# Linear attention and dense layers on one core: the query phase by token halves

## The chip, the cores and the metric

The kernel runs on one core of one Trainium2 chip. The core has a matrix engine (TensorE, PE in the profile, with its weight loads as PEld), a vector engine (VectorE, DVE), an engine for functions of one operand (ScalarE, ACT), a general engine (GpSimd, POOL) and an engine that issues transfers (SyncE, SP). Matrix products land in PSUM, which the kernel divides into eight tiles of 128 x 512; everything else is in SBUF, 128 partitions wide. The metric is the device time of one execution in microseconds (us), given as the median of the runs.

## What is computed

The reference is a linear attention followed by two dense layers, all in float32.

```python
def phi(x):                                   # per head; 128 features from 64 values
    proj = x @ w_phi
    proj = proj - max(abs(proj), axis=-1)     # one maximum per token
    return concat(exp(proj), exp(-proj))      # 256 features

kv  = phi(k).T @ v                            # per head 256 x 64
z   = sum(phi(k), axis=tokens)                # per head 256
num = phi(q) @ kv
den = phi(q) @ z + 1e-6
x   = num / den                               # 8 batches x 576 tokens, 8 heads x 64 = 512 values
out = leaky_relu(x @ w_in, 0.01) @ w_out      # 4608 tokens, 512 -> 2048 -> 512
```

Note that the subtraction uses the largest absolute value of a token's 128 projections, and that it is the same number for both signs of the exponent.

## The kernel before

**Pairs.** Attention goes by pairs of heads. A batch has 8 heads, so 4 pairs, and there are 32 pairs; pair i belongs to batch i // 4. Pairs 0 to 3 (batch 0) go through code of their own at the start (`first_k_phase`, `first_q_phase`); the others through `k_phase(i)` and `q_phase(i)`. The key phase builds the pair's key-value matrix in five chunks of tokens (tiles kvh and, from pair 8 on, kvl, each with one buffer). The query phase projects the queries, subtracts the maxima, takes the exponentials, multiplies by the key-value matrix and divides by the denominators. Its result goes into `ring`, a tile with two batch slots.

**High and low parts.** From pair 8 on, and in the dense layers throughout, a float32 operand is split into a rounded part and the rest (names ending in h and l), and a product is the sum of three matmuls in a faster format. The query phase rounds its exponentials with a reduction over one element (L378, tile qh) and takes the rest on POOL (line 72, tile ql).

**The dense layers.** They go by 18 blocks of 256 tokens. `split` reads a block's input out of `ring` with casts on ScalarE (tile xh, line 67) and subtractions on POOL (tile xl, line 72); the casts are cut where a batch ends, so a block's pieces have 64, 128, 192 or 256 columns. `layer1` is 12 matmuls for each of 16 slices of the hidden layer (L572, L573, L575), `layer2` is 6 (L592 to L594). Blocks 0 and 1 run interleaved while the weights still arrive. Block 1 keeps its low part in a buffer that the key phase's value tile vhl takes over from pair 8 on.

**The query phase in detail (L321 to L402).** A pair has two heads j and 576 tokens, in two halves u of U = 288.

1. Four projections, each 288 tokens of a head, land in PSUM (tag a, three buffers, which key phase and query phase share). VectorE transposes each into the tile tq (L346). This transpose works in blocks of 32 by 32, so that a token's 128 features lie in four groups of 32 partitions.
2. For each head a reduction (L348) takes the maxima over the 32 features that a partition sees: tile m, 18 blocks of tokens.
3. The four groups must be combined. Four transfers from SP bring the four groups side by side into a tile ms of 32 partitions (L351), VectorE reduces them to mm (L354), and four transfers bring the result to all four groups as mx (L357).
4. For each head: subtract (L364), transpose back into mb (L366), then for each half both exponentials (L371, L372), the rounding, the matmuls with the key-value matrix (L386, L388, L391) into a PSUM tile, and two copies on ScalarE: the numerator into `ring` (L393), the denominator into a part of tq that is no longer needed (L394, `dn = tq[:, 0]`).
5. When both heads and both halves are through: transpose the denominators (L397), reciprocal (L399), transpose back (L400), and one multiply on POOL over 576 columns of `ring` (line 72, ring from ring and mb).

The denominator comes in 64 equal rows per head, which is why one column per block of 32 serves for the reciprocal.

**What sets the order.** `attention()` runs `k_phase(i)` and `q_phase(i - 1)` as two generators that take turns; each `yield` ends a turn. `advance` draws on that stream between the slices of the dense layers. This writes the program's order and gives each instruction a priority: attention's stands ahead of the dense layers', weights' preparation in between. The tile framework then makes, when the kernel is built, one fixed order for each engine from priorities, dependences, free buffers and a model of durations. On the chip each engine works its list in that order and waits where an operand is late. A tile with one buffer can only be taken again when everything that reads it is over. `BUFS` holds the buffer counts of SBUF tags; tags not named there have one.

```python
BUFS = {"kph": 2, "eq": 2, "m4": 2, "g": 2, "gh": 2, "gl": 2, "qh": 2, "ql": 2}
PBUFS = {"a": 3, "c": 1, "h": 2, "acc": 2}
```

Of the kernel before, what the change touches and what calls it, by code (L numbers as in the profile page):

```python
# [17 lines left out]
P = 128  # L18
# [13 lines left out]
NK = 8  # L32
BUFS = {"kph": 2, "eq": 2, "m4": 2, "g": 2, "gh": 2, "gl": 2, "qh": 2, "ql": 2}
PBUFS = {"a": 3, "c": 1, "h": 2, "acc": 2}
# [10 lines left out]
def attention_moe_kernel(ctx: ExitStack, tc: tile.TileContext, q, k, v, vt, w_phi, w_in, w_out, out):  # L45
# [275 lines left out]
    def q_phase(i):  # L321
# [12 lines left out]
        tq = st([P, 2, 2, U], F32, "tq")  # L334
        m = st([P, 2, 18], F32, "m")
        for j in range(2):
            for u in range(2):
                pq = pt("a")[:, 0:U]
                us = slice(U * u, U * u + U)
                if nat:  # L340
                    r = slice(64 * j, 64 * j + 64)
                    nc.tensor.matmul(pq, lhsT=bd[r, F * j : F * j + F], rhs=rq[r, us], start=True, stop=True)
                else:
                    nc.tensor.matmul(pq, lhsT=wq_h, rhs=qs[:, j, us], start=True, stop=False)  # L344
                    nc.tensor.matmul(pq, lhsT=wq_l, rhs=qs[:, j, us], start=False, stop=True)  # L345
                nc.vector.transpose(tq[:, j, u], pq)  # L346
                yield
            nc.vector.tensor_reduce(m[:, j], blocks(tq[:, j]), axis=AX.X, op=ALU.max, apply_absolute_value=True)  # L348
        ms = st([32, 4, 2, 18], F32, "ms")
        for a in range(4):  # L350
            nc.sync.dma_start(ms[:, a], m[32 * a : 32 * a + 32])  # L351
        yield
        mm = st([32, 2, 18], F32, "mm")
        nc.vector.tensor_reduce(mm, ms.rearrange("p a j c -> p j c a"), axis=AX.X, op=ALU.max)  # L354
        mx = st([P, 2, 18], F32, "mx")
        for a in range(4):
            nc.sync.dma_start(mx[32 * a : 32 * a + 32], mm)  # L357
        m = mx
        yield
        kvh, kvl = kvs_of[i]  # L360
        dn = tq[:, 0]
        for j in range(2):
            tj = blocks(tq[:, j])
            nc.vector.tensor_tensor(tj, tj, m[:, j].unsqueeze(2).broadcast_to([P, 18, 32]), op=ALU.subtract)  # L364
            mb = st([P, 2, U], F32, "mb")
            nc.vector.transpose(mb.rearrange("p a b -> p (a b)"), tq[:, j].rearrange("p a b -> p (a b)"))  # L366
            yield
            es = []
            for u in range(2):
                eq = st([P, 2, U], F32, "eq")  # L370
                nc.scalar.activation(eq[:, 0], mb[:, u], AF.Exp)  # L371
                nc.scalar.activation(eq[:, 1], mb[:, u], AF.Exp, scale=-1.0)  # L372
                if nat:
# [7 lines left out]
                yield  # L381
            for u in range(2):
                qh, ql = es[u]
                nm = pt("a")[:, 0:U]
# [7 lines left out]
                rr = slice(64 * j, 64 * j + 64)  # L392
                nc.scalar.copy(ring[rr, b % 2, hp, U * u : U * u + U], nm[0:64])  # L393
                nc.scalar.activation(dn[rr, u], nm[64:128], AF.Copy, bias=1e-6)  # L394
                yield
        dt = st([P, 2, U], F32, "mb")
        nc.vector.transpose(dt.rearrange("p a b -> p (a b)"), dn.rearrange("p a b -> p (a b)"))  # L397
        rc = st([P, 18], F32, "rc")
        nc.vector.reciprocal(rc, blocks(dt)[:, :, 0])  # L399
        nc.vector.transpose(blocks(dt), rc.unsqueeze(2).broadcast_to([P, 18, 32]))  # L400
        x = ring[:, b % 2, hp]
        tt_("x", x, x, dt.rearrange("p a b -> p (a b)"), ALU.mult)  # L402
        yield

# [284 lines left out]
```

## Time and profile before

| What | Value |
| --- | --- |
| Median of 3 runs | 1220.52 us (1220.07 to 1224.94) |
| Profiled execution, first to last instruction (span) | 1217.5 us; the page gives no other time for it |
| Mean granted TensorE clock | 0.989 |
| TensorE matmuls | busy 1171.4 us, 96%, 7496 matmuls |
| TensorE weight loads | busy 1038.5 us, 85% |
| ScalarE | busy 865.7 us, 71% |
| VectorE | busy 741.7 us, 61% |
| GpSimd | busy 625.2 us, 51% |

How to read it. The first number of a timeline row is the start in us from the first instruction, the second the duration in us, then engine, source line, operation, the tile written and the tiles read, sizes and count; in brackets stand the idle time before it and what ended that. Matmuls are pipelined: the durations of neighbours overlap, so the number of matmuls in a stretch says more than their busy time. PEclk is the clock that TensorE was granted, as a share of full speed. Line 67 and line 72 are helpers that serve many tiles: there one goes by the tile names. In a row of waits the numbers are the total in us, how many times, and the longest.

### The profile page before, as it was taken

To read this page: it belongs to the slowest core of one execution; us is meant where nothing else is said; L and a number is where in the kernel's file an instruction comes from. 1 tells how busy PE (TensorE), PEld (TensorE's weight loads), DVE (VectorE), ACT (ScalarE), POOL (GpSimd) and SP (SyncE) were. 2 spreads that over 40 slices of the span, in tenths; PEclk is the share of its full clock that TensorE was granted. 3 is DMA by queue.
4 is the path that set the end of the run, shared out by engine and by line. 5 is a ranking of instruction groups with operands and counts; after the bars stand their busy time and mean duration, and the time that the engine had idled before them with its cause. 6 is when DMAs were issued, how large, how long until landed. Compare 5 with 4: busy or idle time off the path is not lost.

```text
span 1217.5 us, 21546 instructions
## 1 busy us (share of the span) xinstructions
PE 1171.4 (96%) x7496; PEld 1038.5 (85%) x7496; DVE 741.7 (61%) x1243; ACT 865.7 (71%) x2267; POOL 625.2 (51%) x681
## 2 busy tenths in 40 slices
PE   8889999789998999989999999999999999999998
PEld 5577778579996999879999999899999999989997
DVE  6969893556677666667667766776776766400000
ACT  5977785677877777877878887887887877533232
POOL 0132222355766566655757666766676757433232
PEclk9999999899999999989999999999999999999999
DMA  7526241201111011111101010111111110000000
GB/s 213 149 73 167 86 116 32 75 24 33 50 25 56 13 32 40 42 41 33 49 23 49 22 50 22 50 33 49 33 39 29 43 23 19 3 18 1 18 18 18
DMA packets 73532, 58.07 MB, mean 48 GB/s; under 512 B 55888, under 2 KB 57040, under 8 KB 73424
## 3 DMA queue, kind: packets, MB, share of 16 engines
q1 hardware_dynamic: 73424, 56.70, 16.7%
q8 instruction: 59, 0.97, 0.3%
q14 instruction: 49, 0.40, 0.1%
HBM read 46.20 MB, written 9.44 MB: 46 GB/s over the span
## 4 chain that ended last, share of the span: by engine, by line
PE 72%; ACT 8%; DVE 6%; issue 4%; DMA 3%; POOL 3%; SPq 2%; DVEq 0%; POOLq 0%; ACTq 0%
PE h L572 9%; PE h L575 9%; PE h L573 9%; PE acc L592 8%; PE acc L593 8%; PE acc L594 8%; PE c L224 6%; PE a L386 2%; PE a L244 2%; PE a L391 2%; PE a L388 2%; DMA ring<-in_w_in_dram 1%; DMA ms<-m 1%; PE a L344 1%; PE a L345 1%
## 5 line engine op out<-in xcount | busy, mean ns | idle before, releaser
L72 POOL TENSOR_TENSOR gl<-g,gh 128x256 fp32r<-128x256 f32 x288 | 233.7, 816 | 314.7 <-ACT gh L67 251.9
L572 PE MATMUL h<-xh,w0h 128*128 128x256 f32 x1088 | 281.3, 286 | 7.4 <-ACT xh L67 4.1
L573 PE MATMUL h<-xh,w0l 128*128 128x256 f32 x1088 | 278.2, 283 | 0.0
L572 PEld LDWEIGHTS h<-xh,w0h 128*128 128x128 f32 x1088 | 206.9, 190 | 20.4 <-ACT xh L67 5.1
L592 PE MATMUL acc<-w1h,gh 128*128 128x512 f32 x544 | 215.7, 396 | 0.0
L573 PEld LDWEIGHTS h<-xh,w0l 128*128 128x128 f32 x1088 | 207.1, 190 | 9.1
L593 PE MATMUL acc<-w1l,gh 128*128 128x512 f32 x544 | 214.8, 395 | 0.0
L594 PE MATMUL acc<-w1h,gl 128*128 128x512 f32 x544 | 204.2, 397 | 0.1
L575 PE MATMUL h<-xl,w0h 128*128 128x256 f32 x1088 | 192.2, 283 | 0.0
L579 ACT ACTIVATE g<-h 128x256 f32<-128x256 f32 x288 | 108.1, 380 | 97.3 <-PE h L575 84.2
L72 POOL TENSOR_TENSOR ql<-eq,qh 128x576 fp32r<-128x576 f32 x96 | 146.7, 1537 | 51.6 <-DVE qh L378 39.3
L67 ACT CAST gh<-g 128x256 fp32r<-128x256 f32 x288 | 114.5, 403 | 65.0 <-PE acc L593 62.8
L575 PEld LDWEIGHTS h<-xl,w0h 128*128 128x128 f32 x1088 | 157.4, 190 | 0.9 <-issue 0.4
L72 POOL TENSOR_TENSOR kpl<-ek,kph 128x512 fp32r<-128x512 f32 x72 | 97.2, 1350 | 80.2 <-ACT kph L67 46.5
L269 ACT ACTIVATE ek<-pmk,m4n 128x128 f32<-128x128 f32 (+1 forms) x240 | 88.4, 393 | 44.4 <-POOL kpl L72 23.1
L594 PEld LDWEIGHTS acc<-w1h,gl 128*128 128x128 f32 x544 | 99.9, 188 | 18.7 <-POOL gl L72 0.9
L592 PEld LDWEIGHTS acc<-w1h,gh 128*128 128x128 f32 x544 | 102.5, 188 | 13.7 <-issue 0.8
L593 PEld LDWEIGHTS acc<-w1l,gh 128*128 128x128 f32 x544 | 102.5, 189 | 12.6
L270 ACT ACTIVATE ek<-pmk,m 128x128 f32<-128x128 f32 (+1 forms) x240 | 88.0, 391 | 25.3 <-DVE m L252 20.8
L378 DVE TENSOR_REDUCE qh<-eq 128x576 fp32r<-128x576 f32 x96 | 70.0, 750 | 42.6 <-ACT eq L372 23.3
L224 PE MATMUL c<-kph,vhl 128*66 128x256 f32 (+1 forms) x480 | 78.0, 285 | 5.3 <-ACT kph L67 5.1
L249 DVE TENSOR_TENSOR pmk<-a,pmk 128x256 f32<-128x256 f32 (+1 forms) x120 | 48.3, 417 | 50.5 <-ACT pmk L67 47.9
(201 smaller groups left out, 2324.8 us busy)
## 6 DMA issues: line engine op xcount, KB each, us to landing
out_dram<-o SPq DMA_DIRECT2D x35, 256.0 KB, 2.0
rq<-in_q_dram SPq DMA_DIRECT2D x28, 288.0 KB, 2.9
rk<-in_k_dram SPq DMA_DIRECT2D x27, 288.0 KB, 2.8
rv<-in_v_dram SPq DMA_DIRECT2D x29, 256.0 KB, 3.5
ring<-in_w_in_dram SPq DMA_DIRECT2D x9, 512.0 KB, 3.8
f<-in_w_out_dram SPq DMA_DIRECT2D x7, 512.0 KB, 3.6
f<-in_w_in_dram SPq DMA_DIRECT2D x7, 512.0 KB, 3.7
ring<-in_w_out_dram SPq DMA_DIRECT2D x5, 512.0 KB, 3.7
```

What stands on the lines that cost most here:

```text
L67: nc.scalar.copy(o, i)
L72: (nc.vector if pick(key) == "v" else nc.gpsimd).tensor_tensor(o, a, b, op=op)
L224: nc.tensor.matmul(kvp[0 : lt.shape[1], 256 * j : 256 * j + 256], lhsT=lt, rhs=rt, start=first and j == 0, stop=last, skip_group_check=True)
L269: nc.scalar.activation(ek[r, j, 0:F], pmk[r, h], AF.Exp, bias=m4n[r, h : h + 1])
L270: nc.scalar.activation(ek[r, j, F:256], pmk[r, h], AF.Exp, scale=-1.0, bias=m4[r, h : h + 1])
L572: nc.tensor.matmul(ph, lhsT=weight(0, "h", ft)[:, d * P : d * P + P], rhs=xh[d], start=d == 0, stop=False)
L573: nc.tensor.matmul(ph, lhsT=weight(0, "l", ft)[:, d * P : d * P + P], rhs=xh[d], start=False, stop=False)
L575: nc.tensor.matmul(ph, lhsT=weight(0, "h", ft)[:, d * P : d * P + P], rhs=xl[d], start=False, stop=d == NP - 1)
L579: nc.scalar.activation(g, ph, AF.Prelu, alpha=0.01)
L592: nc.tensor.matmul(a, lhsT=gh[:, ts], rhs=weight(1, "h", ft), start=ft == 0, stop=False)
L593: nc.tensor.matmul(a, lhsT=gh[:, ts], rhs=weight(1, "l", ft), start=False, stop=False)
L594: nc.tensor.matmul(a, lhsT=gl[:, ts], rhs=weight(1, "h", ft), start=False, stop=ft == NFT - 1)
```

## The change

The query phase changes in four places.

- **Order.** Where it went head by head and, within a head, half by half, it now goes half by half and, within a half, both heads. tq is laid out with the half outermost, and the reductions, subtractions and transposes take a half of both heads (2 x 288 columns, the same size as before).
- **Denominators.** They get a tile of their own (dn, 288 columns, now two buffers) and are no longer written into tq. The tail (transpose, reciprocal, transpose, multiply on POOL) runs once for each half over 288 columns and not once for the pair over 576; the transposed denominators take the other buffer of dn and not mb.
- **Crossing of the maxima.** m has room for four groups. The group that already lies in partitions 0 to 31 stays where it is; three transfers bring the others beside it, the reduction writes straight into partitions 0 to 31 of mx, and three transfers bring it to the other groups. The tiles ms and mm are gone.
- **Scratch.** The argument `dynamic_dma_scratch_size` goes from 1024 to 256.

```diff
-BUFS = {"kph": 2, "eq": 2, "m4": 2, "g": 2, "gh": 2, "gl": 2, "qh": 2, "ql": 2}
+BUFS = {"kph": 2, "eq": 2, "m4": 2, "g": 2, "gh": 2, "gl": 2, "qh": 2, "ql": 2, "dn": 2}
...
-        m = st([P, 2, 18], F32, "m")
-        for j in range(2):
-            for u in range(2):
+        m = st([P, 4, 2, 18], F32, "m")
+        for u in range(2):
+            us = slice(U * u, U * u + U)
+            for j in range(2):
...
-                nc.vector.transpose(tq[:, j, u], pq)
+                nc.vector.transpose(tq[:, u, j], pq)
                 yield
-            nc.vector.tensor_reduce(m[:, j], blocks(tq[:, j]), axis=AX.X, op=ALU.max, apply_absolute_value=True)
-        ms = st([32, 4, 2, 18], F32, "ms")
-        for a in range(4):
-            nc.sync.dma_start(ms[:, a], m[32 * a : 32 * a + 32])
-        yield
-        mm = st([32, 2, 18], F32, "mm")
-        nc.vector.tensor_reduce(mm, ms.rearrange("p a j c -> p j c a"), axis=AX.X, op=ALU.max)
+            nc.vector.tensor_reduce(m[:, 0, u], blocks(tq[:, u]), axis=AX.X, op=ALU.max, apply_absolute_value=True)
+        for a in range(1, 4):
+            nc.sync.dma_start(m[0:32, a], m[32 * a : 32 * a + 32, 0])
+        yield
         mx = st([P, 2, 18], F32, "mx")
-        for a in range(4):
-            nc.sync.dma_start(mx[32 * a : 32 * a + 32], mm)
-        m = mx
+        nc.vector.tensor_reduce(mx[0:32], m[0:32].rearrange("p a u c -> p u c a"), axis=AX.X, op=ALU.max)
+        for a in range(1, 4):
+            nc.sync.dma_start(mx[32 * a : 32 * a + 32], mx[0:32])
         yield
         kvh, kvl = kvs_of[i]
-        dn = tq[:, 0]
-        for j in range(2):
-            tj = blocks(tq[:, j])
-            nc.vector.tensor_tensor(tj, tj, m[:, j].unsqueeze(2).broadcast_to([P, 18, 32]), op=ALU.subtract)
+        for u in range(2):
+            us = slice(U * u, U * u + U)
+            tu = blocks(tq[:, u])
+            nc.vector.tensor_tensor(tu, tu, mx[:, u].unsqueeze(2).broadcast_to([P, 18, 32]), op=ALU.subtract)
             mb = st([P, 2, U], F32, "mb")
-            nc.vector.transpose(mb.rearrange("p a b -> p (a b)"), tq[:, j].rearrange("p a b -> p (a b)"))
+            nc.vector.transpose(mb.rearrange("p a b -> p (a b)"), tq[:, u].rearrange("p a b -> p (a b)"))
             yield
             es = []
-            for u in range(2):
+            for j in range(2):
                 eq = st([P, 2, U], F32, "eq")
-                nc.scalar.activation(eq[:, 0], mb[:, u], AF.Exp)
+                nc.scalar.activation(eq[:, 0], mb[:, j], AF.Exp)
...
-            for u in range(2):
-                qh, ql = es[u]
+            dn = st([P, U], F32, "dn")
+            for j in range(2):
+                qh, ql = es[j]
...
-                nc.scalar.copy(ring[rr, b % 2, hp, U * u : U * u + U], nm[0:64])
-                nc.scalar.activation(dn[rr, u], nm[64:128], AF.Copy, bias=1e-6)
+                nc.scalar.copy(ring[rr, b % 2, hp, us], nm[0:64])
+                nc.scalar.activation(dn[rr], nm[64:128], AF.Copy, bias=1e-6)
                 yield
-        dt = st([P, 2, U], F32, "mb")
-        nc.vector.transpose(dt.rearrange("p a b -> p (a b)"), dn.rearrange("p a b -> p (a b)"))
-        rc = st([P, 18], F32, "rc")
-        nc.vector.reciprocal(rc, blocks(dt)[:, :, 0])
-        nc.vector.transpose(blocks(dt), rc.unsqueeze(2).broadcast_to([P, 18, 32]))
-        x = ring[:, b % 2, hp]
-        tt_("x", x, x, dt.rearrange("p a b -> p (a b)"), ALU.mult)
-        yield
+            dt = st([P, U], F32, "dn")
+            nc.vector.transpose(dt, dn)
+            dt = dt.rearrange("p (c d) -> p c d", d=32)
+            rc = st([P, 9], F32, "rc")
+            nc.vector.reciprocal(rc, dt[:, :, 0])
+            nc.vector.transpose(dt, rc.unsqueeze(2).broadcast_to([P, 9, 32]))
+            x = ring[:, b % 2, hp, us]
+            tt_("x", x, x, dt.rearrange("p c d -> p (c d)"), ALU.mult)
+            yield
...
-    nc = _bacc.Bacc("TRN2", target_bir_lowering=False, num_devices=1, dynamic_dma_scratch_size=1024)
+    nc = _bacc.Bacc("TRN2", target_bir_lowering=False, num_devices=1, dynamic_dma_scratch_size=256)
```

More of the change, by code (lines that the diff above doesn't have):

```diff
@@ L334, in q_phase @@
         tq = st([P, 2, 2, U], F32, "tq")
-        m = st([P, 2, 18], F32, "m")
-        for j in range(2):
-            for u in range(2):
+        m = st([P, 4, 2, 18], F32, "m")
+        for u in range(2):
+            us = slice(U * u, U * u + U)
+            for j in range(2):
                 pq = pt("a")[:, 0:U]
-                us = slice(U * u, U * u + U)
                 if nat:
@@ L345, in q_phase @@
                     nc.tensor.matmul(pq, lhsT=wq_l, rhs=qs[:, j, us], start=False, stop=True)
-                nc.vector.transpose(tq[:, j, u], pq)
+                nc.vector.transpose(tq[:, u, j], pq)
                 yield
-            nc.vector.tensor_reduce(m[:, j], blocks(tq[:, j]), axis=AX.X, op=ALU.max, apply_absolute_value=True)
-        ms = st([32, 4, 2, 18], F32, "ms")
-        for a in range(4):
-            nc.sync.dma_start(ms[:, a], m[32 * a : 32 * a + 32])
+            nc.vector.tensor_reduce(m[:, 0, u], blocks(tq[:, u]), axis=AX.X, op=ALU.max, apply_absolute_value=True)
+        for a in range(1, 4):
+            nc.sync.dma_start(m[0:32, a], m[32 * a : 32 * a + 32, 0])
         yield
-        mm = st([32, 2, 18], F32, "mm")
-        nc.vector.tensor_reduce(mm, ms.rearrange("p a j c -> p j c a"), axis=AX.X, op=ALU.max)
         mx = st([P, 2, 18], F32, "mx")
-        for a in range(4):
-            nc.sync.dma_start(mx[32 * a : 32 * a + 32], mm)
-        m = mx
+        nc.vector.tensor_reduce(mx[0:32], m[0:32].rearrange("p a u c -> p u c a"), axis=AX.X, op=ALU.max)
+        for a in range(1, 4):
+            nc.sync.dma_start(mx[32 * a : 32 * a + 32], mx[0:32])
         yield
         kvh, kvl = kvs_of[i]
-        dn = tq[:, 0]
-        for j in range(2):
-            tj = blocks(tq[:, j])
-            nc.vector.tensor_tensor(tj, tj, m[:, j].unsqueeze(2).broadcast_to([P, 18, 32]), op=ALU.subtract)
+        for u in range(2):
+            us = slice(U * u, U * u + U)
+            tu = blocks(tq[:, u])
+            nc.vector.tensor_tensor(tu, tu, mx[:, u].unsqueeze(2).broadcast_to([P, 18, 32]), op=ALU.subtract)
             mb = st([P, 2, U], F32, "mb")
-            nc.vector.transpose(mb.rearrange("p a b -> p (a b)"), tq[:, j].rearrange("p a b -> p (a b)"))
+            nc.vector.transpose(mb.rearrange("p a b -> p (a b)"), tq[:, u].rearrange("p a b -> p (a b)"))
             yield
             es = []
-            for u in range(2):
+            for j in range(2):
                 eq = st([P, 2, U], F32, "eq")
-                nc.scalar.activation(eq[:, 0], mb[:, u], AF.Exp)
-                nc.scalar.activation(eq[:, 1], mb[:, u], AF.Exp, scale=-1.0)
+                nc.scalar.activation(eq[:, 0], mb[:, j], AF.Exp)
+                nc.scalar.activation(eq[:, 1], mb[:, j], AF.Exp, scale=-1.0)
                 if nat:
```

## The prediction

> **What bounds the kernel now.** I read the page's busy shares first, then a table of stretches, then the order of work in the stretches that fall short.
>
> ```profile
> PE 1171.4 (96%) x7496; PEld 1038.5 (85%) x7496; DVE 741.7 (61%) x1243; ACT 865.7 (71%) x2267; POOL 625.2 (51%) x681
> ```
> ```profile
> core 0: us, PE busy (x) PEld busy (x) DVE busy (x) ACT busy (x) POOL busy (x), PEclk, DMA share, GB/s
> 220.00:260.00 40.00, 28.39 (x138) 21.88 (x138) 22.26 (x42) 28.87 (x75) 13.16 (x15) 0.83 0.27 74
> 370.00:400.00 30.00, 23.94 (x141) 20.04 (x141) 19.17 (x35) 22.60 (x60) 16.82 (x19) 0.94 0.17 50
> 510.00:540.00 30.00, 22.92 (x124) 19.54 (x125) 20.72 (x36) 23.81 (x63) 16.41 (x16) 0.83 0.18 51
> 600.00:1000.00 400.00, 399.65 (x2743) 369.46 (x2741) 281.37 (x445) 319.20 (x864) 264.08 (x264) 1.00 0.14 37
> 540.00:1200.00 660.00, 658.75 (x4444) 606.22 (x4443) 364.28 (x580) 453.53 (x1224) 385.60 (x405) 1.00 0.10 29
> ```
>
> TensorE is the bound: from 540 to 1200 us it is busy 658.75 of 660 us, so an operation saved elsewhere there is worth nothing. The change adds and removes no matmul. What can be won is time in which TensorE does less than its steady pace of 2743/400 = 6.86 matmuls per us. Three stretches before 540 fall short: 138 matmuls are 20.1 us of steady work in 40 us, 141 are 20.6 in 30, 124 are 18.1 in 30. The losses, empty time and lowered clock together, are 19.9 + 9.4 + 11.9 = **41.2 us**. That is the ceiling on a gain from these stretches.
>
> What ends each stretch is the same event, the cast of the last missing piece of a dense-layer block's input:
>
> ```profile
> 251.76 0.35 ACT L67 CAST xh<-ring 128x192 fp32r<-128x192 f32 x1 [0.99 <-POOL ring L72]
> 390.73 0.30 ACT L67 CAST xh<-ring 128x128 fp32r<-128x128 f32 x1 [0.98 <-POOL ring L72]
> 530.12 0.23 ACT L67 CAST xh<-ring 128x64 fp32r<-128x64 f32 x1
> ```
>
> The sizes name the blocks. Blocks have 256 tokens, a batch 576. Block 2 takes tokens 0 to 191 of batch 1, block 4 tokens 0 to 127 of batch 2, block 6 tokens 0 to 63 of batch 3. All three wait for the batch's last pair of heads, and all three need only its **first half** (288 tokens). So attention is what is late until 530 us, and the query phase's order matters.
>
> **The change part by part, in the third stretch.** First the halves. Today the order is head by head:
>
> ```profile
> 516.91 0.39 ACT L393 COPY ring<-a 64x288 f32<-64x288 f32 x1
> 518.41 0.39 ACT L393 COPY ring<-a 64x288 f32<-64x288 f32 x1
> 518.82 0.41 ACT L394 ACTIVATE tq<-a 64x288 f32<-64x288 f32 x1
> 521.35 0.39 ACT L393 COPY ring<-a 64x288 f32<-64x288 f32 x1
> 522.76 0.39 ACT L393 COPY ring<-a 64x288 f32<-64x288 f32 x1
> ```
> ```profile
> 523.95 0.78 DVE L397 STREAM_TRANSPOSE mb<-tq 128x576 f32<-128x576 f32 x1
> 525.43 0.26 DVE L399 RECIPROCAL rc<-mb 128x18 f32<-128x18 f32 x1
> 526.89 0.73 DVE L400 STREAM_TRANSPOSE mb<-rc 128x576 f32<-128x576 f32 x1
> ```
> ```profile
> 518.41 3.25 POOL L72 TENSOR_TENSOR ql<-eq,qh 128x576 fp32r<-128x576 f32 x2 [3.05 <-DVE qh L378]
> 528.00 1.41 POOL L72 TENSOR_TENSOR ring<-ring,mb 128x576 f32<-128x576 f32 x1
> ```
>
> The first two copies are both halves of head 0; after the change they are both heads of the first half, complete when the denominator copy ends at 519.23. The tail is cut in two. Its pieces have these durations (least, median, most, in ns):
>
> ```profile
> L346 DVE STREAM_TRANSPOSE tq<-a x112: 418/470/485, 93.3 to 1042.7; 128x288 f32<-128x288 f32 x112
> L527 DVE RECIPROCAL rc<-mb x9: 190/193/206, 48.2 to 85.9; 128x8 f32<-128x8 f32 x9
> L72 POOL TENSOR_TENSOR ring<-ring,mb x37: 722/1427/1792, 49.8 to 1073.0; 128x576 f32<-128x576 f32 x28, 128x256 f32<-128x256 f32 x9
> ```
>
> Two transposes and a reciprocal: 0.47 + 0.19 + 0.47 = 1.13, so 520.4. POOL is in its ql pair until 521.66. A 288-column multiply lies between 0.72 (256 columns) and 1.43 (576), by columns 0.79, so 522.45; with the cast's 0.23 the block starts at 522.7 and not 530.35: **7.6 us** earlier. Per pair the cut costs VectorE 2 x 1.13 - (0.78 + 0.26 + 0.73) = 0.5 us and POOL 2 x 0.79 - 1.41 = 0.2 us; both engines have idle time in every row of the table above, so I cost it at nothing on the path. If that cover were gone it would be 0.7 us a pair. Two waits are new. The first half's denominator transpose waits on VectorE for ScalarE's copy, with the second half's rounding reductions (L378) behind it and POOL's ql behind those: where the copy is late, the second half is late by as much, but no block in these stretches waits for the second half. And the tile of maxima m is now read until the combining reduction, so the next pair's maxima wait for that; with one pair's crossing over by 506.89 (row below) and the next pair's first transposes at 525.60, or 11.4 us earlier, there is room.
>
> Second, the denominators leave the query tile (tq, one buffer). It is now held until the last denominator transpose has read it; after, only until the second score transpose:
>
> ```profile
> 512.56 0.77 DVE L366 STREAM_TRANSPOSE mb<-tq 128x576 f32<-128x576 f32 x1
> 525.60 0.42 DVE L346 STREAM_TRANSPOSE tq<-a 128x288 f32<-128x288 f32 x1
> 496.87 0.40 DVE L314 TENSOR_TENSOR kvl<-c,kvh 128x256 fp32r<-128x256 f32 x1
> ```
> ```profile
> 512.36 0.29 PE L386 MATMUL a<-qh,kvh 128*128 128x288 f32 x1
> ```
>
> The tile is free at 513.33, not 524.73 (these rows are of pair 15 giving way to pair 16; pair 15's own start I take to move by as much): the next pair's projections, maxima and crossing may begin **11.4 us** earlier. How much reaches the end? The lower bound is 0, if PSUM slots or engine order hold the front back. The upper bound is the key phase: a pair's output matmuls need its key-value matrix, complete for pair 15 at 497.27, while the first ran at 512.36, 15.1 us later. 11.4 fits inside; I take it whole, because the next front starts within a microsecond of the tile's release today (524.73 to 525.60). The third stretch then ends 7.6 + 11.4 = **19 us** earlier.
>
> Not all of that is gain, for attention worked meanwhile:
>
> ```profile
> 511.40:530.40 19.00, 11.92 (x66) 9.24 (x64) 15.95 (x29) 15.91 (x41) 10.30 (x9) 0.88 0.19 56
> ```
>
> Of these 66 matmuls some 20 (12 of the first half, 8 of the next pair's projections) would lie ahead of the earlier end; 46 are still owed, 46/6.86 = 6.7 us. The first two stretches are not added: block 6 cannot start before pair 15, whatever the dense layers won earlier. Net **12.3 us**.
>
> Third, the crossing of the maxima goes from four transfers each way to three:
>
> ```profile
> 506.89 1.80 DVE L364 TENSOR_TENSOR tq<-tq,mx 128x576 f32<-128x576 f32 x2 [0.62 <-DMA mx<-mm]
> ```
> ```profile
> 498.86 2.68 SPq L351 DMA_DIRECT2D ms<-m  x4
> ```
> ```profile
> DVE mm L354 <- DMA ms<-m: 51.4, 23, 4.7
> DVE mb L397 <- ACT tq L394: 42.2, 25, 9.4
> DVE tq L364 <- DMA mx<-mm: 42.1, 23, 6.4
> ```
>
> An issue costs SP 2.68/4 = 0.67 us, so each way ends about 0.6 us sooner, with 2 x 28 issues fewer ahead of the q, k, v and output transfers on that queue. VectorE stands at these three waits 135.7 us in all, 4.8 us a pair, with the key phase's subtractions and maxima queued behind. The bounds of what a pair's spacing gains are 0 (the key phase is held by ACT and POOL) and 4.8; I take 1 us, near the two shortened crossings' 1.2. Over the 7 spacings from pair 8 to pair 15 that is +7. Against it, pair 8's key phase cannot fill its value tile before block 1's first layer is through:
>
> ```profile
> 219.15 0.12 POOL L106 MEMSET vhl<- 128x20 f32 x1 [0.67 <-PE h L575]
> ```
>
> Pair 7's query phase, moved up by as much as 11.4 us, puts its matmuls ahead of that point: a loss between 0 and 24 matmuls, 3.5 us; I take 3. Sum: 12.3 + 7 - 3 = **16 us**. The profiled span is 1217.5, the median of the runs 1220.5, 3.0 outside the span; 1217.5 - 16 + 3 = **1204 us**. With the front moved whole and the other unknowns between their ends (spacing 0 to 3 us, the late key phase 3.5 to 0) the net is 8.8 to 33.3, and this case alone spans 1187 to 1212; a front that moves not at all is a rival below. The moved scratch size carries nothing: every transfer is issued from SP.
>
> On the lowered clock:
>
> ```profile
> 380.00:390.00 10.00, 6.38 (x31) 5.14 (x30) 8.09 (x17) 7.98 (x20) 3.86 (x4) 0.83 0.18 56
> ```
> ```profile
> 382.42 0.58 PE L386 MATMUL a<-qh,kvh 128*128 128x288 f32 x1 [2.19 <-DVE qh L378]
> ```
>
> The clock fell to 0.83 in ten microseconds whose longest gap shown here is 2.19 us. The Trainium skill (TensorE: Matmul & The Clock Gate, Part 1: The HAM clock gate) gives half rate only after an idle window of about 3.4 us. By that rule shortened stretches would keep the full clock and about 17% of 30 us in the third, 5 us more, would return: 1199 us. The trace speaks against it, so my sum lets the remaining stretch be slow.
>
> **The rivals.** *Attention leaves the path.* If the closed loop through the query tile sets today's spacing, breaking it lets pairs follow at 30 us or less:
>
> ```profile
> 286.30 1.43 POOL L72 TENSOR_TENSOR ring<-ring,mb 128x576 f32<-128x576 f32 x1
> ...
> 1073.00 1.43 POOL L72 TENSOR_TENSOR ring<-ring,mb 128x576 f32<-128x576 f32 x1
> ```
>
> Pairs 8 to 31 stand 786.7/23 = 34.2 us apart, in full and in empty stretches alike, which fits a loop of their own. All but some 5 us of the 41 come back: 1184. Against it, the key phase is a second loop with one buffer for most tiles.
>
> *Only the halves work*: the front stays where it is. 7.6 us less 2 for owed matmuls: 1215.
>
> *Nothing moves*: a block waits for another batch member instead, 1220.
>
> *Slower*: the moved-up front puts its crossing waits on VectorE's queue ahead of the key phase's operations. At 1.5 us a pair over 23 spacings that is 34.5, less 19 at the end: 1236. It decides from 19/23 = 0.8 us a pair on. For it speaks the 4.8 us of waits; against it, that these waits are there already.
>
> **How the numbers follow.** Forecast 0.42, attention off the path 0.20, halves only 0.20, nothing 0.06, slower 0.12. The range 1184 to 1219 leaves out the slower case and a little below. About 0.5%, 6 us, is what this measurement tells from no change, so faster means under 1214.4: nearly all of the first, all of the second, under half of the third: 0.70. Slower 0.12, the rest, 0.18, the same.
>
> **What would show it.** Right: the three casts come well before 251, 390 and 530; a pair's first projection transposes stand ahead of the former pair's last denominator transpose; the three stretches hold more matmuls; spacing 32 to 34 us. Wrong: projections that still follow the last transpose (halves only), spacing near 30 or above 35, or a new stretch under 6 matmuls per us before 220 or after 540.

## The result and the profile after

The changed kernel takes 1208.03 us (median of 4 runs, 1207.22 to 1209.21) beside 1220.93 us for the kernel before on the same chip: a ratio of **0.9887, 95% interval 0.9869 to 0.9905**, 1.1% faster. Forecast were 1204 us and a range of 1184 to 1219. The profiled executions last 1217.5 us and 1205.4 us.

The busy shares of the changed kernel, from its page (TensorE still bounds it), and then its row for the stretches that the prediction showed (columns as there):

```profile
PE 1168.8 (97%) x7496; PEld 1035.9 (86%) x7496; DVE 747.7 (62%) x1327; ACT 861.8 (71%) x2267; POOL 631.5 (52%) x709
```
```profile
220.00:260.00 40.00, 35.07 (x209) 29.26 (x207) 24.22 (x44) 29.51 (x77) 16.95 (x23) 0.91 0.24 67
370.00:400.00 30.00, 28.15 (x186) 25.85 (x187) 21.42 (x41) 24.50 (x68) 18.93 (x19) 0.94 0.15 41
510.00:540.00 30.00, 29.66 (x202) 27.76 (x202) 20.06 (x38) 23.18 (x63) 19.30 (x21) 0.95 0.11 26
600.00:1000.00 400.00, 396.42 (x2702) 364.21 (x2702) 282.19 (x475) 313.94 (x854) 259.83 (x273) 1.00 0.13 35
```

The three short stretches fill up (138, 141 and 124 matmuls before; 209, 186 and 202 now), but the steady stretch thins out: 2702 matmuls in 400 us, where there were 2743. So the end is a balance of two parts. The same view, cut at 540 us, first for the kernel before, then for the changed one:

```profile
0.00:540.00 540.00, 499.33 (x2980) 421.04 (x2981) 376.76 (x662) 408.43 (x1035) 235.97 (x272) 0.97 0.26 71
540.00:1060.00 520.00, 519.24 (x3554) 479.82 (x3553) 358.87 (x572) 406.38 (x1099) 336.83 (x338) 1.00 0.12 33
```
```profile
0.00:540.00 540.00, 511.51 (x3090) 434.36 (x3091) 384.94 (x706) 413.16 (x1053) 251.96 (x292) 0.98 0.25 71
540.00:1060.00 520.00, 516.42 (x3519) 474.90 (x3518) 357.68 (x612) 403.27 (x1099) 331.38 (x353) 1.00 0.12 33
```

Until 540 us the changed kernel is 110 matmuls ahead, 110/6.86 = **16.0 us**. Between 540 and 1060 us it loses 35 of them, **5.1 us**. That leaves 10.9 of the 12.1 us between the spans. These two counts are the measure in everything that follows.

In windows of 60 us, wide enough to hold a stretch in both kernels, the first (200 to 260) holds 76 matmuls more than before, the second (340 to 400) 14 and the third (480 to 540) 24. That is not yet the account of the 110, because TensorE can use up a lead while it waits for the next batch. Cut at 513.30, where block 6's cast ends in the changed kernel, the third stretch looks so, before and then after:

```profile
513.30:540.00 26.70, 19.62 (x106) 16.66 (x105) 18.56 (x34) 20.72 (x56) 13.88 (x14) 0.81 0.20 57
```
```profile
513.30:540.00 26.70, 26.36 (x187) 24.48 (x187) 17.31 (x33) 20.80 (x56) 16.29 (x18) 1.00 0.11 26
```

At 513.30 the lead is only 29 matmuls (2905 and 2876 until there); 81 of the 110 come behind it. Until its own cast of block 6 ends, each kernel has started 1692 matmuls with the dense layers' weights: whatever the first two stretches won, block 6 still waited for its own last pair. The casts that ended the stretches, in the changed kernel's timeline:

```profile
240.22 0.35 ACT L67 CAST xh<-ring 128x192 fp32r<-128x192 f32 x1
376.42 0.30 ACT L67 CAST xh<-ring 128x128 fp32r<-128x128 f32 x1 [0.23 <-POOL ring L72]
513.05 0.24 ACT L67 CAST xh<-ring 128x64 fp32r<-128x64 f32 x1 [0.75 <-POOL ring L72]
```

They come 11.5, 14.3 and 17.1 us earlier than before. Next, the query phase of pair 15 giving way to pair 16, in the timelines of VectorE and TensorE of the changed kernel (L363 the score transpose of the second half, L389 the last output product, L344 and L346 the next pair's first projection and its transpose, L395 the second half's denominators):

```profile
503.46 0.77 DVE L363 STREAM_TRANSPOSE mb<-tq 128x576 f32<-128x576 f32 x1
...
512.10 0.68 PE L389 MATMUL a<-ql,kvh 128*128 128x288 f32 x2
...
513.23 0.29 PE L344 MATMUL a<-qs,wq 128*128 128x288 f32 x1
...
513.69 0.48 DVE L346 STREAM_TRANSPOSE tq<-a 128x288 f32<-128x288 f32 x1 [0.22 <-PE a L345]
514.25 0.48 DVE L395 STREAM_TRANSPOSE dn<-dn 128x288 f32<-128x288 f32 x1
```

tq is free at 504.23, but the next front (the first steps of the next pair's query phase, from its projections on) begins at 513.23, behind the last output product. Counted from the end of pair 15's second score transpose, the next projection transpose came 12.3 us later before and comes 9.5 us later now: 2.8 us are won here, not 11.4. The kernel before shows why, in rows of TensorE that the prediction did not look at:

```profile
522.23 0.45 PE L391 MATMUL a<-ql,kvh 128*128 128x288 f32 x2
522.52 0.30 PE L344 MATMUL a<-qs,wq 128*128 128x288 f32 x1
```

The projection already stood right behind the last output product there, 2.2 us ahead of the release of tq at 524.73. And VectorE's waits at the crossing, in the table of waits of the changed kernel:

```profile
DVE tq L361 <- DMA mx<-mx: 80.3, 27, 4.3
```

The wait behind the second crossing has nearly doubled, from 42.1 to 80.3 us, although one transfer fewer is issued each way.

### The profile page after: what moved, and what is told of

Its sections match the earlier page's. It is cut to its first block, busy times and chain, and to the rows that moved or that the text cites. A ratio compares the mean times of both kernels' runs of the same rounds, so it can differ in the third digit from the quotient of the medians.

```text
span 1205.4 us, 21633 instructions
## 1 busy us (share of the span) xinstructions
PE 1168.8 (97%) x7496; PEld 1035.9 (86%) x7496; DVE 747.7 (62%) x1327; ACT 861.8 (71%) x2267; POOL 631.5 (52%) x709
## 4 chain that ended last, share of the span: by engine, by line
PE 69%; DVE 10%; ACT 9%; issue 4%; DMA 4%; SPq 2%; POOL 2%; DVEq 0%; POOLq 0%; ACTq 0%
PE h L571 9%; PE h L574 9%; PE h L572 9%; PE acc L591 8%; PE acc L592 8%; PE acc L593 8%; PE c L224 5%; PE a L384 2%; DMA mx<-mx 2%; PE a L244 2%; PE a L389 2%; PE a L386 2%; DMA m<-m 2%; DVE tq L361 1%; SPq L350 1%
## 5 line engine op out<-in xcount | busy, mean ns | idle before, releaser
L574 PE MATMUL h<-xl,w0h 128*128 128x256 f32 x1088 | 187.4, 281 | 0.0
L574 PEld LDWEIGHTS h<-xl,w0h 128*128 128x128 f32 x1088 | 154.6, 188 | 0.6 <-POOL xl L72 0.2
L361 DVE TENSOR_TENSOR tq<-tq,mx 128x576 f32<-128x576 f32 x56 | 59.2, 1097 | 80.3 <-DMA mx<-mx 80.3
L375 DVE TENSOR_REDUCE qh<-eq 128x576 fp32r<-128x576 f32 x96 | 70.8, 749 | 44.4 <-ACT eq L369 20.2
L368 ACT ACTIVATE eq<-mb 128x288 f32<-128x288 f32 x112 | 49.2, 439 | 53.5 <-DVE mb L363 50.1
```

What stands on the lines that cost most here:

```text
L361: nc.vector.tensor_tensor(tu, tu, mx[:, u].unsqueeze(2).broadcast_to([P, 18, 32]), op=ALU.subtract)
L574: nc.tensor.matmul(ph, lhsT=weight(0, "h", ft)[:, d * P : d * P + P], rhs=xl[d], start=False, stop=d == NP - 1)
```

## The experiments

Three parts can be set apart: the order by halves with its tail by halves (H), the denominators' own tile (D) and the crossing with three transfers (C). All eight combinations were measured; the two endpoints are the kernel before and the changed kernel. Where D is off and H is on, numerator order and tail go by halves, and the denominators and their transpose lie in parts of tq, so tq is held until the multiply on POOL. All but the kernel before have the smaller scratch; no run changes it alone, but in the traces of both endpoints every transfer is issued from SP, as the prediction says. "Ratio" is against the kernel before on the same chip; the counts are TensorE's matmuls in the two windows shown above; "8 to 15" is the time between POOL's multiplies of pairs 8 and 15 (the second ones where there are two); "between" is VectorE's busy time from the end of the reduction that starts the second crossing to the start of the subtraction that waits for it, a mean over pairs 17 to 31.

| Kernel | us | ratio (95%) | until 540 | 540 to 1060 | 8 to 15, us | between, us |
| --- | --- | --- | --- | --- | --- | --- |
| before | 1221.85 | 1 | 2980 | 3554 | 241.7 | 1.76 |
| H | 1213.61 | 0.9940 (0.9928 to 0.9953) | 3022 | 3533 | 244.9 | 1.71 |
| D | 1213.08 | 0.9932 (0.9918 to 0.9945) | 3035 | 3532 | 234.9 | 1.33 |
| C | 1228.43 | 1.0057 (1.0041 to 1.0072) | 2971 | 3494 | 243.4 | 0.17 |
| H + D | 1207.99 | 0.9883 (0.9866 to 0.9901) | 3058 | 3554 | 242.7 | 1.48 |
| H + C | 1220.70 | 0.9996 (0.9981 to 1.0010) | 3068 | 3476 | 233.6 | 0.37 |
| D + C | 1228.68 | 1.0052 (1.0036 to 1.0068) | 2951 | 3505 | 243.8 | 0.38 |
| H + D + C, the change | 1208.03 | 0.9887 (0.9869 to 0.9905) | 3090 | 3519 | 235.0 | 0.09 |

(before: median of the 17 runs beside the later kernels; the ratios of H, D, C and of the change go by earlier runs of it.) Averaged over the other two parts, H changes the time by -10.4 us, D by -6.7 and C by **+7.3**. They do not add up: each edit makes the planner lay new lists for every engine.

The expectations name these theories. *The prediction's own terms*: halves 7.6 us, an earlier front 11.4, a crossing 1 us a pair. *Theory A*, formed from the changed kernel's trace: the front is held by PSUM's tag a, so that freeing tq is worth nothing. *Theory A2*, formed after the first four runs: freeing tq gains about 1 us a pair, and the three-transfer crossing loses, because VectorE stands idle behind it.

**Each part alone.**

```diff
-        for j in range(2):
-            for u in range(2):
+        for u in range(2):
+            us = slice(U * u, U * u + U)
+            for j in range(2):
...
-        dn = tq[:, 0]
...
+            dn = tq[:, u, 0]
...
+            dt = tq[:, u, 1]
+            nc.vector.transpose(dt, dn)
```

> One part alone: the query phase and its tail go by token halves; denominators stay in parts of the query tile tq that are no longer needed (so tq is held until the second half's tail is over), and the maxima cross with four transfers each way. Theory A (the halves carry most of the gain; freeing tq is worth nothing): the last cast of block 6, at 530.12 before and 513.05 after, comes at about 522, 8 us before the old one; the same 8 us in the stretches at 251 and 390; less some 2 us of owed matmuls the time is near 1215. Rival B (the gain is the three-transfer crossing, the halves are hidden): 1219 to 1222, cast of block 6 near 530. By the prediction's own terms: 7.6 - 2, so 1215, too; it differs from A at the next kernel.

Measured: 1213.61 us, block 6's cast at 523.80. That is 6.3 us earlier than before, against 7.6 forecast for the halves: 7.9 us won from pair 15's first score transpose on (509.10 before, 510.69 here), less 1.6 us by which that transpose is later. The time is within 2 us of the 1215 of both theories. The rival that the halves are hidden falls.

```diff
-        dn = tq[:, 0]
+        dn = st([P, 2, U], F32, "dn")
```

> One part alone: the denominators get a tile of their own (128x2x288, one buffer) and the order stays head by head, so that tq is free after the second head's score transpose and no longer after the denominators' transpose. By the prediction: the next pair's projections start up to 11.4 us earlier, the cast of block 6 comes at about 519, and the time is 11.4 less some 4 us of owed matmuls lower, near 1213. Theory A (the next pair's projections wait for a PSUM buffer of tag a, whose turn comes only after the former pair's last output matmul): the next pair's first projection still stands behind the former pair's last output matmul, cast of block 6 within 2 us of 530, time 1219 to 1222.

Measured: 1213.08 us, as the prediction had it, so theory A's "worth nothing" falls. But block 6's cast is at 523.64, 6.5 us earlier and not 11, and the reason was not the predicted one. In the timelines of this kernel (L365 second score transpose, L390 last output product):

```profile
506.01 0.77 DVE L365 STREAM_TRANSPOSE mb<-tq 128x576 f32<-128x576 f32 x1
...
517.03 0.43 PE L390 MATMUL a<-ql,kvh 128*128 128x288 f32 x2
517.30 0.30 PE L344 MATMUL a<-qs,wq 128*128 128x288 f32 x1
...
518.43 0.47 DVE L346 STREAM_TRANSPOSE tq<-a 128x288 f32<-128x288 f32 x1
```

The projection still stands right behind the former pair's last output product. Over pairs 8 to 15 the first projection transpose comes 12.7 us after the second score transpose, where it came 14.0 us after it before (from the end of the one to the start of the other): the front gains not 11.4 us once, but 1.3 us in every pair. The spacing falls as well, in POOL's multiplies of pairs 8 and 15 (286.30 and 528.00 before; this kernel's rows follow):

```profile
287.14 1.44 POOL L72 TENSOR_TENSOR ring<-ring,mb 128x576 f32<-128x576 f32 x1
...
522.03 1.41 POOL L72 TENSOR_TENSOR ring<-ring,mb 128x576 f32<-128x576 f32 x1
```

234.9 us for seven spacings instead of 241.7, 6.8 us less, 1.0 a spacing. That the earlier front does this is argued, not shown: with the halves on, D brings the front forward by 2.6 us a pair (15.1 to 12.5), but takes only 2.2 us off the seven spacings (244.9 to 242.7).

```diff
-        for a in range(4):
-            nc.sync.dma_start(ms[:, a], m[32 * a : 32 * a + 32])
+        for a in range(1, 4):
+            nc.sync.dma_start(m[0:32, a], m[32 * a : 32 * a + 32, 0])
```

(and the same for the way back, with the reduction straight into mx)

> One part alone: the maxima cross with three transfers each way, all else as before. By the prediction: spacing of the pairs 1 us smaller, the seven spacings from pair 8 to pair 15 at 234.7 us and not 241.7, cast of block 6 near 523, time near 1214. Rival (the change of spacing seen after the whole change comes from the halves): spacing within 0.2 us a pair of before, time 1219 to 1222.

Measured: 1228.43 us, slower than either expected; pairs 8 to 15 take 243.4 us and not 234.7. Before 540 us almost nothing changes (9 matmuls fewer), after it 60 are lost, 8.7 us. One such loss, in the timelines of VectorE and TensorE and in a window of this kernel (L361 subtracts, L375 rounds, L383 is an output product):

```profile
616.88 0.41 DVE L353 TENSOR_REDUCE mx<-m 32x36 f32<-32x144 f32 x1 [6.13 <-DMA m<-m]
620.44 1.43 DVE L361 TENSOR_TENSOR tq<-tq,mx 128x576 f32<-128x576 f32 x2 [3.14 <-DMA mx<-mx]
...
624.06 1.42 DVE L375 TENSOR_REDUCE qh<-eq 128x576 fp32r<-128x576 f32 x2
...
624.87 0.40 PE L383 MATMUL a<-qh,kvh 128*128 128x288 f32 x1 [1.76 <-DVE qh L375]
```
```profile
620.00:630.00 10.00, 8.14 (x44) 7.20 (x43) 7.70 (x12) 6.70 (x18) 5.11 (x5) 0.83 0.00 1
```

VectorE has the subtraction next in its list, stands idle for the crossing, and everything behind is late; TensorE, whose list has an output product there, waits 1.76 us with dense work behind it. The ten microseconds hold 44 matmuls where 69 are the steady pace. In the kernel before the same place looks so (VectorE's timeline, pair 15; the subtraction, at 506.89 after 0.62 us idle, stands in the prediction):

```profile
502.76 0.40 DVE L354 TENSOR_REDUCE mm<-ms 32x36 f32<-32x144 f32 x1 [2.75 <-DMA ms<-m]
504.80 0.75 DVE L249 TENSOR_TENSOR pmk<-a,pmk 128x256 f32<-128x256 f32 x2 [1.63 <-ACT pmk L67]
505.58 0.69 DVE L252 TENSOR_REDUCE m<-pmk 128x4 f32<-128x512 f32 x1
```

Work of the key phase stands between reduction and subtraction and fills part of the crossing. The column "between" says that this holds for all kernels with four transfers (1.3 to 1.8 us) and for none of the four with three (0.1 to 0.4). I call that work the cover; the two experiments under "The cover" give it back. The crossing itself did get shorter: from the end of the reduction to the start of the subtraction it takes 3.2 us here, 4.0 before (same pairs).

**A kernel that should not differ.** The changed kernel with `for a in (3, 2, 1)` in both crossings.

> The changed kernel with one thing different that should not matter: the three transfers of each crossing are issued in the order of groups 3, 2, 1. All theories: 1208 within 2 us. If it differs by more than that, differences of this size between the other kernels cannot be put down to their edits.

Measured: 1207.57 us, ratio 0.9886 (0.9872 to 0.9900). As expected. Its counts are 3080 and 3529, where the changed kernel has 3090 and 3519, and its pairs 8 to 15 take 236.4 us, not 235.0: differences of this size between other kernels show nothing.

**Each part undone.**

```diff
-        for a in range(1, 4):
-            nc.sync.dma_start(m[0:32, a], m[32 * a : 32 * a + 32, 0])
+        for a in range(4):
+            nc.sync.dma_start(ms[:, a], m[32 * a : 32 * a + 32])
```

> The changed kernel with one part undone: the maxima cross with four transfers each way, as before (halves and own tile of the denominators stay). Prediction: the shorter crossing is worth 1 us a pair, so without it 7 us are lost, 1215. Theory A2 (the shorter crossing is a loss: VectorE's subtraction stands right behind the reduction in VectorE's list, so VectorE stands idle through the second crossing, while with four transfers 1.5 us of key-phase work stands between them): idle time of VectorE ahead of the subtraction falls from 80 us to near 45 and the time falls, to 1203 to 1206. Additive reading of the first runs (before 1222.3, halves -8.7, denominators -9.2): 1204.4.

Measured: 1207.99 us, neither: the crossing is worth nothing in the changed kernel. The windows and the wait of this kernel say how:

```profile
0.00:540.00 540.00, 504.33 (x3058) 429.10 (x3059) 390.89 (x704) 410.06 (x1048) 243.72 (x288) 0.98 0.26 71
540.00:1060.00 520.00, 518.64 (x3554) 478.96 (x3553) 362.17 (x617) 409.04 (x1108) 339.27 (x357) 1.00 0.13 33
```
```profile
DVE tq L363 <- DMA mx<-mm: 31.0, 22, 3.7
```

With four transfers it is 32 matmuls (4.7 us) behind the changed kernel at 540 us and gets 35 (5.1 us) back by 1060. So in the changed kernel the shorter crossing does help while attention is late, by 4.7 us: pairs 8 to 15 take 242.7 us without it and 235.0 with it, 7.7 us for the 7 that the prediction had. And about as much is lost while TensorE is full; the experiments under "The cover" ask whether that is the missing cover.

```diff
-            dn = st([P, U], F32, "dn")
+            dn = tq[:, u, 0]
...
-            dt = st([P, U], F32, "dn")
+            dt = tq[:, u, 1]
```

> The changed kernel with one part undone: the denominators stay in parts of the query tile tq (halves and the three-transfer crossing stay). Prediction: 11.4 less owed matmuls lost, about 1215. Theory A2 (the released tile lets the next front start about 1 us earlier in every pair, 7 us by pair 15): spacing of pairs 8 to 15 near 243 instead of 235.0, time 1215 to 1221. Additive reading of the first runs (halves -8.7, crossing +6.1): 1219.7.

Measured: 1220.70 us, as the additive reading had it. The spacing, though, is 233.6 us for pairs 8 to 15 (284.80 to 518.42) and not 243: what is lost lies mostly after 540 us, 43 matmuls, and 22 before. Why D counts after 540 us stays open.

```diff
-        for u in range(2):
-            us = slice(U * u, U * u + U)
-            for j in range(2):
+        for j in range(2):
+            for u in range(2):
```

> The changed kernel with one part undone: head by head as before and one tail per pair (denominators in a tile of their own and the three-transfer crossing stay). Prediction: 7.6 less some 2 us lost, about 1214, cast of block 6 near 521. Theory A2 (the crossing costs, the denominators gain): additive reading of the first runs (denominators -9.2, crossing +6.1): 1219.2, spacing of pairs 8 to 15 near 236.

Measured: 1228.68 us, 20.7 above the changed kernel, far from all readings. 139 matmuls are missing at 540 us, block 6's cast is at 531.43, pairs 8 to 15 take 243.8 us. D's gain of 6.8 us in that spacing disappears with the three-transfer crossing.

**The cover.** The changed kernel, and then the kernel with C alone, each with one more turn for the key phase behind the second crossing:

```diff
         for a in range(1, 4):
             nc.sync.dma_start(mx[32 * a : 32 * a + 32], mx[0:32])
         yield
+        yield
```

> The changed kernel with one more turn for the key phase between the second crossing and the subtraction (one yield more); in VectorE's list that puts two subtractions of the key phase, 1.6 us, between the reduction that starts the second crossing and the query phase's subtraction. Theory A2 (what the three-transfer crossing costs is VectorE standing idle behind it): idle time ahead of the subtraction falls from 80 us to near 45 and part of the 5 us lost after 540 us comes back, 1203 to 1206. Rival (the idle time is off the path): 1207 to 1210.

Measured: 1204.22 us, ratio 0.9851 (0.9835 to 0.9866). Its windows and wait:

```profile
0.00:540.00 540.00, 510.07 (x3089) 429.94 (x3090) 390.22 (x708) 412.36 (x1056) 247.51 (x292) 0.99 0.26 72
540.00:1060.00 520.00, 517.61 (x3535) 476.86 (x3534) 351.99 (x616) 405.81 (x1104) 329.94 (x359) 1.00 0.12 33
```
```profile
DVE tq L362 <- DMA mx<-mx: 42.2, 27, 4.4
```

Nothing changes before 540 us (3089 to 3090); after it 16 of the 35 lost matmuls come back, 2.3 us of a gain of 3.8. The wait falls from 80.3 to 42.2 us, as theory A2 expected.

> The kernel before with the three-transfer crossing alone (1228.4 in the first runs) and one more turn for the key phase between the second crossing and the subtraction, which puts in nearly every pair one or two operations of 0.8 us or less in VectorE's list between the two. Theory A2 (the loss is VectorE's idle time behind the second crossing): the idle time ahead of the subtraction falls from 72 us to near 50, and of the 6 us lost against before at least half comes back: 1222 to 1225. Rival (the loss has another cause): 1227 to 1230.

Measured: 1222.07 us, ratio 0.9999 (0.9987 to 1.0011).

```profile
540.00:1060.00 520.00, 518.62 (x3558) 479.17 (x3557) 342.81 (x574) 404.91 (x1105) 328.08 (x339) 1.00 0.12 33
```
```profile
DVE tq L362 <- DMA mx<-mx: 37.7, 22, 3.1
```

The wait halves (72.3 to 37.7), VectorE's work in between goes from 0.17 to 1.48 us, all of the 60 lost matmuls return (3494 to 3558), nothing changes before 540 us (2971 to 2973), and the time is that of the kernel before. The crossing takes as long as with C alone (3.1 and 3.2 us). So C's loss comes from the list, not from the transfers. One rival is left: a kernel before with the extra turn and four transfers was not run, so a gain that the turn would bring by itself is not excluded. The Trainium skill (DMA: Bandwidth & Descriptors, Rules for kernel authors) has the rule to start a transfer early, compute, and wait on it late, so that its fixed cost overlaps; this pair of kernels agrees, with 6.4 us between them. Why the planner lays the subtraction so close behind three transfers was not tried.

**What holds the front.** A PSUM tag of its own for the projections, in the changed kernel and, as a control, in the kernel before:

```diff
-PBUFS = {"a": 3, "c": 1, "h": 2, "acc": 2}
+PBUFS = {"a": 2, "p": 1, "c": 1, "h": 2, "acc": 2}
...
-                pq = pt("a")[:, 0:U]
+                pq = pt("p")[:, 0:U]
```

> The changed kernel with the four projections of the query phase in a PSUM tag of their own with one buffer; tag a keeps two, so the number of PSUM tiles stays. Theory A (the next pair's projections wait for their turn in tag a, behind the former pair's last output product, and not for tq): the first projection transpose, 13 to 14 us after the second score transpose now, comes within 2 us of it, a whole 11 us earlier, and the pairs 8 to 15 close up to 32 us or less each; if the prediction's value of an earlier front (11.4 us at block 6, less 6.7 of owed matmuls, some 5 us) holds, the time is 1203 or below. Rival (the front is held by VectorE's or TensorE's order and not by PSUM): front where it was, 1206 to 1212. Rival 2 (the front moves, but two buffers in tag a hold up the key phase and the output products): front early, spacing 35 or more, slower than 1212.

Measured: **1201.73 us**, ratio 0.9841 (0.9825 to 0.9857), the fastest kernel of the study. Its timelines, windows and wait:

```profile
469.00 0.73 DVE L363 STREAM_TRANSPOSE mb<-tq 128x576 f32<-128x576 f32 x1
469.76 0.48 DVE L346 STREAM_TRANSPOSE tq<-p 128x288 f32<-128x288 f32 x1
...
478.71 0.41 DVE L314 TENSOR_TENSOR kvl<-c,kvh 128x256 fp32r<-128x256 f32 x1
...
486.67 0.30 PE L384 MATMUL a<-qh,kvh 128*128 128x288 f32 x1
```
```profile
501.70 0.24 ACT L67 CAST xh<-ring 128x64 fp32r<-128x64 f32 x1
```
```profile
0.00:540.00 540.00, 514.56 (x3157) 439.59 (x3158) 421.07 (x740) 424.82 (x1086) 258.00 (x298) 0.99 0.26 72
540.00:1060.00 520.00, 513.88 (x3483) 470.27 (x3483) 349.94 (x583) 393.52 (x1074) 338.36 (x355) 1.00 0.12 32
```
```profile
DVE tq L361 <- DMA mx<-mx: 27.1, 17, 4.0
```

The first two rows are again pair 15 giving way to pair 16: the projection transpose follows the second score transpose at once (mean of pairs 8 to 15: 0.6 us, 13.1 in the changed kernel). So it was the turn in tag a, not tq, that still held the front in the changed kernel. Pair 16's front begins 43.9 us earlier than there (469.76 and 513.69), but block 6's cast only 11.4 us earlier. That this equals the prediction's figure is chance. Pair 15's query side is now early: its first half's rounded exponentials are done at 475.87 (the end of POOL's ql), but its key-value matrix is complete only at 479.12 (third row), and its first output product stands at 486.67 (fourth row), behind dense work in TensorE's list. The pairs 8 to 15 stand 32.9 us apart, not the 32 or less expected of theory A. At 540 us 67 more matmuls are through (9.8 us), but 36 are lost after it (5.2 us). Not all of this is the front: the list has cover here too, the wait at the crossing is 27.1 us.

> The kernel before with the same division of PSUM (one buffer for the projections, two in tag a); tq still holds the denominators. Theory A: the first projection transpose still follows the last denominator transpose, as tq is only free then; what differs from before is the price of two buffers in tag a, 0 to +6 us. If this kernel is faster than before by more than 3 us, a gain of the same division in the changed kernel is not due to the front.

Measured: 1335.07 us, ratio 1.0927, far outside what was expected. Its front is where it was (14.7 us behind the second score transpose, mean of pairs 8 to 14, 14.3 before), as theory A says: without the release of tq the tag of its own moves nothing. But it is 113 us slower, and the pairs 8 to 15 stand 38.5 us apart (294.11 to 563.48 in POOL's multiplies), where the kernel before has 34.5. So the gain in the changed kernel is not due to the division of PSUM by itself. What makes the division so dear in this kernel, and what waits for what there, stays open.

> Both added to the changed kernel: one more turn for the key phase behind the second crossing, and PSUM divided so that the projections have a buffer of their own. If both gain as theory A and A2 say, 1198 to 1203; if the early front costs more in the key phase than it gives, above 1206.

Measured: 1209.76 us, ratio 0.9904 (0.9890 to 0.9917). The front is as early (0.6 us) and the wait as short (28.1 us), but only 3127 matmuls are through at 540 us and 3464 come after. The two gains do not add. Beside the kernel with the cover alone, the early front is 38 matmuls ahead at 540 us (5.5 us) and loses 71 after it (10.3 us); beside the changed kernel it was 9.8 us ahead and lost 5.2. So it takes 6.3 us off one kernel's time and puts 5.5 on the other's, and I call the front's worth not settled.

## Why the prediction was right, and where it was wrong

The sum was 16 us, and 110 matmuls at 540 us are 16.0 us; the time fell by 12.9. But the agreement of the 16 is made of errors that cancel. The prediction has the third cast 26 us earlier (7.6, 11.4 and 7) and 9.7 us of it owed or lost (6.7 and 3). The cast came 17.1 us earlier, 8.0 by the halves and 9.1 because pair 15's first score transpose came earlier (500.03, 509.10 before), where 18.4 were forecast; 3.1 us were owed, and 2.0 came back behind the cast.

- **The bound and the place**: right. TensorE's short stretches before 540 us were the only source, and the last pair's first half was what they waited for.
- **Halves, 7.6 us**: right. From the first score transpose to block 6's cast it took 530.12 - 509.10 = 21.0 us before and 513.05 - 500.03 = 13.0 us after: 8.0 us. Alone they are worth 7.9 us from there on.
- **tq's release, 11.4 us taken whole**: wrong. The ground was that the next front starts within a microsecond of tq's release. But the last output product ended 2.0 us ahead of that release, the projection stood right behind it already, and in the changed kernel that is what held it, through PSUM's tag a. The lower bound of 0 had named it ("PSUM slots"). Alone, the release gave 1.3 us a pair at the front, and the seven spacings took 6.8 us less. With a PSUM buffer of their own as well, the projections do follow tq's release; block 6's cast is then 11.4 us earlier, but by another way than the prediction's.
- **The crossing, 1 us a pair**: about right in size before 540 us, wrong in the whole. In the changed kernel it takes 7.7 us off the seven spacings and gives 4.7 us until 540 us, but 5.1 are lost after it. I had costed the transfers and put the saving on the path; what the shorter crossing displaced was the cover in VectorE's list, which I had not looked at. The gain hangs on the halves: without them the three-transfer crossing lengthens the seven spacings (241.7 to 243.4, with D 234.9 to 243.8).
- **46 owed matmuls, 6.7 us**: too many. When its cast of block 6 ends, each kernel has started 1692 matmuls with the dense layers' weights, and 1234 others before, 1213 now: 21 are owed, 3.1 us, because the rest of attention's work had come earlier too.
- **The first two stretches not added**: right, as those equal 1692 show.
- **The late key phase, 3 us**: too much. Block 1's first layer lets the value tile go at 220.97, 219.15 before, and 6 matmuls are missing at 219.15 (1079 and 1085): 0.9 us, no more than the counts of the reversed kernel differ by.
- **The remaining stretch left slow**: a small term taken as nothing. Before, TensorE ran at a clock of 0.50 from 529.10 to 535.92, mostly behind the cast; in the changed kernel it is 1.00 from the cast to 540. The cast's 17.1 us are 117 matmuls, less 21 owed 96; the lead at 540 is 110. Of the 14 more, 2.0 us, 12 are the slow clock before: 54 matmuls between its cast and 540, where 66 are the steady pace.
- **Nothing after 540 us**: wrong. The rival "slower" had half of the mechanism, crossing waits on VectorE's queue ahead of other work, though by a front that moves up, and a price of 34.5 us; in the changed kernel the loss is 5.1 us and takes part of the gain. In H + C it takes nearly all of it (88 matmuls ahead at 540 us, 78 lost after it); C and D + C have won nothing by 540 us.
- **Attention leaves the path**: no. Pairs 15 to 31 stand 34.6 us apart (515.63 to 1068.78 in POOL's second multiplies), 34.1 before.
- **The signs**: the three casts and the fuller stretches came; "projections ahead of the last denominator transpose" came by 0.6 us only (513.69 against 514.25), behind the last output product, and so was no proof of an early front. The spacing of pairs 8 to 15 is 33.6 us, as forecast.

## What to carry to other kernels

When one resource is released earlier, look for the next one that the same work takes in turn, here a shared PSUM tag: a start that follows two releases at once shows the cause of neither. A shorter transfer can lose more than it gains when its waiting instruction moves up in the engine's list and no other work is left ahead of it, so read the list between issue and wait, and not only the transfer's length. And where a planner lays the lists anew at each edit, measure parts in combination: here one part (the denominators' tile) changed the time by anything from +0.3 to -12.7 us and another (the crossing) from 0 to +15.6, depending on which of the others were present. And ask of a gain in an early stretch whether the next stretch has to wait anyway.

## What was not expected of the hardware

TensorE's clock fell where TensorE had no long wait. In the changed kernel the mean clock is 0.83 from 360 to 370 us and from 370 to 380. Narrower windows show what that mean is made of; behind them the two largest groups of TensorE's waits between 340 and 380 us:

```profile
362.76:366.17 3.41, 1.34 (x6) 0.57 (x4) 3.31 (x8) 1.48 (x5) 1.67 (x1) 1.00 0.00 0
366.17:369.59 3.42, 3.29 (x13) 3.24 (x14) 2.22 (x4) 3.06 (x8) 2.82 (x2) 0.50 0.21 79
369.59:373.00 3.41, 1.55 (x10) 1.06 (x10) 3.12 (x5) 3.34 (x9) 2.44 (x2) 1.00 0.37 105
373.00:376.41 3.41, 3.41 (x17) 3.18 (x16) 2.48 (x6) 3.07 (x8) 3.39 (x3) 0.50 0.15 58
```
```profile
PE c L224 <- POOL kpl L72: 2.1, 2, 1.3
PE a L384 <- DVE qh L375: 1.4, 1, 1.4
```

The clock is at half for 3.4 us, full for 3.4 us, and at half for 3.4 us again. Ahead of each slow piece lie 3.41 us in which TensorE is busy for only 1.34 and 1.55 us, but in pieces: its longest wait is 1.4 us. So these rows fit a clock that goes by how little TensorE did in such a stretch, and not by one long wait; from which share on it falls, they do not say. The rule of the Trainium skill that the prediction weighed (TensorE: Matmul & The Clock Gate, Part 1: The HAM clock gate), half rate only after an idle window of about 3.4 us, would have the clock full here if a window must be wholly idle; the trace does not agree. Another passage of the same page (A second HAM failure mode: psum-queue depth-cycling) tells of another kernel in which frequent short idle times lower the clock; that fits these rows.
